# Down projection of a fused attention and FFN kernel: seven block products per 256 tokens in place of eight

## Chip, cores, metric

One core of one Trainium2 chip. The metric is the device time of that core in microseconds (us). Stage times come from the trace of one profiled execution per kernel.

## What is computed

Causal attention with a bias made from cumulated positions (batch 8, 8 heads, 576 positions, head size 64), whose output is the input of a gated FFN (4608 tokens, model width 512, inner width 1536). Inputs and output are fp32, the kernel computes in bf16. The change concerns the last line:

```python
def _moe_ref(x, w_gate, w_val, w_out):
    g = x @ w_gate
    silu = g * (1.0 / (1.0 + np.exp(-g)))
    val = x @ w_val
    return (silu * val @ w_out).astype(np.float32)
```

## The kernel before

The FFN runs over nine tiles of 512 tokens. A tile has a **gate stage** (twelve blocks of 128 inner columns, each with eight matmuls of 512 columns, a tanh on ScalarE and two VectorE products, `pp` and `ht`) and a **down stage** (four blocks of 128 tokens, each with twelve matmuls of 512 columns). Between the items of both stages (each `yield`) pieces of the attention of the next batch are slipped in: scores, masks on GpSimd, the product with V, casts and DMA issues on GpSimd, and copies of transposed keys and queries on VectorE. Tiles 7 and 8 have no attention left.

```python
        def ffn_items(tt):
            xt = XT[:, :, (tt % 3) * TT : (tt % 3 + 1) * TT]
            hts = []
            ...                                   # stores of the tile before
            for ft in range(NFT):                 # gate stage, NFT = 12
                ...                               # four matmuls into pg; tanh into th
                nc.vector.scalar_tensor_tensor(   # L578
                    pp, in0=th, scalar=1.0, in1=pg, op0=ALU.add, op1=ALU.mult
                )
                give(gbs)
                yield 1
                ...                               # four matmuls into pv
                ht = hpool.tile([128, TT], BF16, tag="ht", bufs=16, name="ht")
                nc.vector.tensor_mul(ht, pp, pv)  # L591
                give(vbs)
                hts.append(ht)
                yield 1
            for ts_ in range(4):                  # down stage
                ...                               # (the last block of all: two halves)
                ybs = take()
                py = view(ybs, DM)
                for ft in range(NFT):
                    nc.tensor.matmul(             # L620
                        py, hts[ft][:, ts_ * 128 : (ts_ + 1) * 128],
                        WO[ft // WKO][:, ft % WKO, :],
                        start=(ft == 0), stop=(ft == NFT - 1),
                    )
                    if ft % 4 == 3 and ft < NFT - 1:
                        yield 1
                ysb = yp.tile([128, DM], FP32, tag="y", name="ysb")
                nc.scalar.mul(ysb, py, 0.5)
                give(ybs)
                ...                               # store, one block late
```

Other work of VectorE and GpSimd in the gate stage that the argument needs:

```python
    split(h + 1, "k", nc.vector)          # keys, queries: copy of a DMA-transposed tile (L278, after: L281)
    cast_one(h + 2, "k", nc.gpsimd)       # 128x1152 fp32 to bf16 (after: L252)
    cast_v(bn, 0, nc.gpsimd)              # 128x512 fp32 to bf16 (after: L179)
    # masks of the scores on GpSimd: affine_select (after: L388, L393)
```

The softmax here doesn't subtract the row's maximum and nothing guards it: scores larger than these inputs give would overflow.

## Time and profile before

| | before |
|---|---|
| median time, three runs | 390.43 us (388.56 to 390.73) |
| span of the profile, granted clock | 388.6 us, 1.000 |
| TensorE, VectorE, GpSimd busy | 96%, 62%, 49% |
| tile 3: gate stage, down stage | 26.94, 13.31 us |
| last matmul to the end | 4.2 us |

A stage is measured from its first matmul to the first matmul of the next. Line numbers differ between the two kernels: L578, L591, L620 before are L605, L621, L668 after. The profile's lines stand in the prediction; the stage of one tile, with busy time (and instructions) of PE, PEld, DVE, ACT and POOL, then granted clock, DMA share and GB/s, is added here for tile 3.

```profile
164.23:191.17 26.94, 26.94 (x236) 14.96 (x232) 20.94 (x37) 16.28 (x33) 17.57 (x30) 1.00 0.83 198
191.17:204.47 13.30, 13.30 (x110) 7.24 (x108) 4.75 (x12) 7.19 (x15) 7.65 (x12) 1.00 0.96 226
```

TensorE has no gap in either stage. VectorE has 6 us free in the gate stage, 8.5 in the down stage.

### The profile page before, as it was taken

Reading aid. Unit: us, or ns where it says so; the run is one execution under the profiler, and the core shown is the slowest. Engines: PE = TensorE matmul, PEld = TensorE weight load, DVE = VectorE, ACT = ScalarE, POOL = GpSimd, SP = SyncE. Lnnn points to the kernel's source line nnn. Section 1 sums busy time; section 2 is a strip of 40 time slices with the busy share of each in tenths; the row PEclk is TensorE's granted clock in tenths of the full one; section 3 lists DMA queues with packets and bytes.
Section 4 is the critical chain, followed back from the end, with each engine's and each line's share of the span. In section 5 each row is a group of like instructions: output and inputs, shape, how many; then the busy total and the mean of one; then the engine's idle time right before and its main releaser. Section 6 shows DMA issues by size and latency. Waiting matters only on the chain.

```text
span 388.6 us, 7949 instructions
## 1 busy us (share of the span) xinstructions
PE 371.3 (96%) x3006; PEld 206.2 (53%) x3006; DVE 239.8 (62%) x431; ACT 214.5 (55%) x411; POOL 192.3 (49%) x329
## 2 busy tenths in 40 slices
PE   3779999999999999999999999999999999999995
PEld 3565556655555555555555555555555544444443
DVE  7676777468653786369735884488347625733750
ACT  7686877567646565566556655565464513323321
POOL 7683368656695756566656666576342220011001
PEclk9999999999999999999999999999999999999999
DMA  7999999996859998996789757964231222002002
GB/s 245 196 244 261 197 264 257 303 254 165 158 153 269 287 221 220 211 267 153 184 215 288 122 178 142 293 159 98 61 113 35 32 73 69 3 27 81 2 12 97
DMA packets 100534, 64.18 MB, mean 165 GB/s; under 512 B 81888, under 2 KB 85824, under 8 KB 100496
## 3 DMA queue, kind: packets, MB, share of 16 engines
q1 hardware_dynamic: 90816, 45.36, 50.3%
q0 software_dynamic: 9680, 18.32, 18.2%
q8 instruction: 23, 0.38, 0.4%
q14 instruction: 15, 0.12, 0.1%
HBM read 37.90 MB, written 19.86 MB: 149 GB/s over the span
## 4 chain that ended last, share of the span: by engine, by line
PE 82%; DVE 6%; DMA 5%; issue 3%; ACT 2%; POOL 0%; DVEq 0%; ACTq 0%; SPq 0%; POOLq 0%
PE bank L571 21%; PE bank L620 21%; PE bank L586 20%; PE bank L367 9%; PE bank L405 6%; DMA pk<-ks 2%; PE wide L367 2%; DVE pp L578 2%; ACT pt L380 1%; DVE ht L591 1%; DVE kq L320 1%; DMA kq<-HL 1%; PE one L405 1%; DMA XT<-xs 1%; DMA s_sb<-in_s_dram 1%
## 5 line engine op out<-in xcount | busy, mean ns | idle before, releaser
L380 ACT ACTIVATE pt<-bank 128x512 bf16<-128x512 f32 x224 | 104.1, 504 | 40.3 <-PE bank L367 28.5
L578 DVE SCALAR_TENSOR_TENSOR pp<-th,bank 128x512 bf16<-128x512 bf16 x108 | 74.1, 686 | 69.8 <-ACT th L576 69.0
L571 PE MATMUL bank<-XT,wg 128*128 128x512 bf16 x432 | 111.0, 379 | 1.1 <-DMA XT<-xs 0.5
L586 PE MATMUL bank<-XT,wv 128*128 128x512 bf16 x432 | 110.9, 379 | 0.2 <-DVE pp L578 0.2
L576 ACT ACTIVATE th<-bank 128x512 bf16<-128x512 f32 x108 | 64.5, 597 | 78.2 <-PE bank L571 73.9
L620 PE MATMUL bank<-wo,ht 128*128 128x512 bf16 x420 | 102.4, 379 | 0.0
L591 DVE TENSOR_TENSOR ht<-pp,bank 128x512 bf16<-128x512 bf16 x108 | 74.0, 685 | 8.8
L367 PEld LDWEIGHTS <-kq 128*128 128x128 bf16 x576 | 46.5, 99 | 40.3 <-issue 6.1
L367 PE MATMUL bank<-kq 128*128 128x128 bf16 (+4 forms) x504 | 65.9, 240 | 0.7 <-DVE ht L591 0.5
L383 POOL TENSOR_SCALAR_AFFINE_SELECT pt<-pt 128x512 bf16<-128x512 bf16 x64 | 41.0, 640 | 34.3 <-ACT pt L380 33.7
L571 PEld LDWEIGHTS <-wg 128*128 128x128 bf16 x432 | 38.3, 98 | 36.6 <-issue 1.2
L586 PEld LDWEIGHTS <-wv 128*128 128x128 bf16 x432 | 38.4, 98 | 35.1 <-issue 1.1
L620 PEld LDWEIGHTS <-ht 128*128 128x128 bf16 x420 | 37.1, 98 | 34.4
L405 PEld LDWEIGHTS <-pt 128*128 128x128 bf16 x960 | 41.5, 98 | 20.7
L439 POOL DMA_DIRECT2D xs<-ot x24 | 21.9, 913 | 60.8 <-DVE ot L422 60.8
L634 POOL DMA_DIRECT2D out_dram<-ysb x35 | 19.7, 562 | 60.9 <-ACT ysb L628 60.9
L628 ACT ACTIVATE ysb<-bank 128x512 f32<-128x512 f32 x35 | 20.9, 597 | 40.9 <-PE bank L620 39.7
L405 PE MATMUL bank<-vt,pt 128*128 128x65 bf16 x840 | 42.8, 194 | 0.0
L190 POOL DMA_DIRECT2D kq<-HL x52 | 31.3, 602 | 2.0 <-PE bank L571 1.6
L421 DVE RECIPROCAL rc<-bank 128x5 f32<-128x5 f32 x56 | 10.6, 190 | 34.4 <-PE bank L405 34.4
L422 DVE TENSOR_TENSOR ot<-bank,rc 128x320 bf16<-128x320 f32 x56 | 27.5, 491 | 1.9
L388 POOL TENSOR_SCALAR_AFFINE_SELECT pt<-pt 128x64 bf16<-128x64 bf16 x64 | 16.4, 256 | 21.3 <-ACT pt L380 21.1
(68 smaller groups left out, 211.1 us busy)
## 6 DMA issues: line engine op xcount, KB each, us to landing
out_dram<-ysb POOLq DMA_DIRECT2D x35, 256.0 KB, 3.3
rawk<-in_k_dram SPq DMA_DIRECT2D x15, 576.0 KB
rawq<-in_q_dram SPq DMA_DIRECT2D x15, 576.0 KB
rawv<-in_v_dram SPq DMA_DIRECT2D x32, 256.0 KB
xs<-ot POOLq DMA_DIRECT2D x24, 160.0 KB, 3.9
ks<-ck SPq DMA_DIRECT2D x11, 288.0 KB
qs<-cq SPq DMA_DIRECT2D x11, 288.0 KB
wg<-in_moe_w_gate_dram POOLq DMA_DIRECT2D x2, 768.0 KB, 11.6
```

Of the source, the lines that this page charges most:

```text
L190: engs[hh].dma_start(KQ[hb % 2][r][r0 : r0 + 4, :, e * S : (e + 1) * S], HL[bh : bh + 1, :, :, :],)
L367: nc.tensor.matmul(sc[:, o : o + w], T[:, 1, e * S + 128 * tj : e * S + 128 * (tj + 1)], T[:, 0, e * S + lo : e * S + hi], start=True, sto ...
L380: nc.scalar.activation(pt[:, c0 : c0 + W], sc[:, 0:W], AF.Exp, scale=0.125)
L383: nc.gpsimd.affine_select(pt[:, 1088:1600], pt[:, 1088:1600], pattern=[[0, 4], [1, 128]], compare_op=ALU.is_ge, fill=zreg, base=0, channel ...
L405: nc.tensor.matmul(av[:, bi * (D + 1) : (bi + 1) * (D + 1)], pt[:, c0 : c0 + 128], VT[b % 2][:, tj, h, :], start=(tj == 0), stop=(tj == bi),)
L422: nc.vector.tensor_mul(ot[:, :, e * D : (e + 1) * D], av3[:, :, 0:D], rc[:, :, None].to_broadcast([128, NCH, D]),)
L571: nc.tensor.matmul(pg, WG[j][:, c, f0 : f0 + 128], xt[:, c, :], start=(c == 0), stop=(c == 3),)
L576: nc.scalar.activation(th, pg, AF.Tanh, scale=0.5)
L578: nc.vector.scalar_tensor_tensor(pp, in0=th, scalar=1.0, in1=pg, op0=ALU.add, op1=ALU.mult)
L586: nc.tensor.matmul(pv, WV[j][:, c, f0 : f0 + 128], xt[:, c, :], start=(c == 0), stop=(c == 3),)
L591: nc.vector.tensor_mul(ht, pp, pv)
L620: nc.tensor.matmul(py, hts[ft][:, ts_ * 128 : (ts_ + 1) * 128], WO[ft // WKO][:, ft % WKO, :], start=(ft == 0), stop=(ft == NFT - 1),)
```

## The change

Each down stage of tiles 1 to 8 is split into two groups of 256 tokens, and each group is a 2x2 block product (token halves by pairs of inner blocks by output halves) done with seven products in place of eight, in Winograd's form of Strassen's scheme. A product is six matmuls of 256 columns. TensorE gets 84 matmuls of 256 columns per tile instead of 48 of 512, an eighth less. The price is sums of operands: of the weights once, of `ht` in every tile (two additions on VectorE, one subtraction in place on GpSimd per pair of blocks), and sums of results.

```diff
+                if k2 == 1 and tt > 0:               # gate stage, after every second ht
+                    su = PTP[0].tile([128, 3, HT], BF16, tag="su", bufs=NP, name="su")
+                    nc.vector.tensor_add(su[:, 0:2, :], hp[:, 0:2, :], hp[:, 2:4, :])         # L628
+                    nc.vector.tensor_add(su[:, 2, :], hp[:, 0, :], hp[:, 3, :])               # L629
+                    nc.gpsimd.tensor_sub(hp[:, 1:3, :], hp[:, 1:4:2, :], hp[:, 0:3:2, :])     # L630
...
+                if ts_ == 3:                          # end of tile 0: sums of the weights
+                    for j in range(2):
+                        weight_sums(j)                # three VectorE operations of 768 elements
+                        weight_differences(j)         # two, in place in WO
...
+        def down_seven(tt, hps, sus):
+            for g in range(2):
+                PB[g] = take()
+                product(P[g][:, 0:HD], True, False, lambda p: hps[p][:, 0, cols], ...)       # raw
+                product(P[g][:, HD:DM], False, False, lambda p: hps[p][:, 3, cols], ...)     # raw
+                nc.scalar.copy(s3, P[g][:, 0:HD])
+                nc.vector.tensor_add(DE[g][:, 0, :], s3, P[g][:, HD:DM])
+                QB[g] = take()
+                product(Q[g][:, HD:DM], True, True, lambda p: hps[p][:, 1, cols], ...)       # difference
+                product(Q[g][:, 0:HD], False, False, lambda p: sus[p][:, 2, cols], ...)      # sum
+                nc.vector.tensor_add(DE[g][:, 1, :], DE[g][:, 0, :], Q[g][:, 0:HD])
+            for g in range(2):
+                product(P[g][:, 0:HD], False, True, lambda p: sus[p][:, 0, cols], ...)
+                product(P[g][:, HD:DM], False, True, lambda p: sus[p][:, 1, cols], ...)
+                nc.scalar.copy(Y[g][:, 1:3, :]..., P[g])
+                nc.gpsimd.tensor_sub(DE[g], DE[g], Y[g][:, 1:3, :])                           # L707
+                product(Q[g][:, 0:HD], False, True, lambda p: hps[p][:, 2, cols], ...)
+                nc.vector.tensor_add(Y[g][:, 0:4:3, :], DE[g], Q[g]...)
+                ...                                   # two stores
...
-    yp = ctx.enter_context(tc.tile_pool(name="yp", bufs=3))
+    yp = ctx.enter_context(tc.tile_pool(name="yp", bufs=2))
```

Cut: the buffers of the scores go from eight to five after the start to make room, and the pace at which attention is slipped in is adapted.

## The prediction

> **What bounds the kernel now.** I read the page's busy lines first, then the chain of work that ended last, then the groups, then VectorE's timeline inside one tile.
>
> ```profile
> PE 371.3 (96%) x3006; PEld 206.2 (53%) x3006; DVE 239.8 (62%) x431; ACT 214.5 (55%) x411; POOL 192.3 (49%) x329
> PE 82%; DVE 6%; DMA 5%; issue 3%; ACT 2%; POOL 0%; DVEq 0%; ACTq 0%; SPq 0%; POOLq 0%
> 342.91 10.36 PE bank L620 x48
> 381.76 2.63 PE bank L604 x24
> ```
>
> The first line is busy time, the second the chain by engine, the last two are pieces of that chain in order of time (start, us, what). TensorE sets the time: its longest waits after the start-up are below 0.6 us in total for each pair of lines. One down projection of a tile (512 tokens) is 48 matmuls of 512 columns in 10.36 us, so 215.8 ns each. The last piece of the last tile, 24 matmuls of 256 columns in 2.63 us, gives 109.6 ns each: a half-width matmul costs half, and the weight loads (98 ns each) stay hidden. So fewer columns on TensorE is the right currency, provided that nothing makes TensorE wait.
>
> ```profile
> L578 DVE SCALAR_TENSOR_TENSOR pp<-th,bank 128x512 bf16<-128x512 bf16 x108 | 74.1, 686 | 69.8 <-ACT th L576 69.0
> L591 DVE TENSOR_TENSOR ht<-pp,bank 128x512 bf16<-128x512 bf16 x108 | 74.0, 685 | 8.8
> 204.60:231.50 26.90, 26.90 (x232) 14.94 (x229) 21.01 (x37) 16.22 (x33) 17.45 (x30) 1.00 0.79 181
> 231.50:244.90 13.40, 13.40 (x110) 7.25 (x108) 5.59 (x12) 7.30 (x16) 7.83 (x13) 1.00 0.88 192
> ```
>
> The last two lines are busy time by engine (PE, PEld, DVE, ACT, POOL) in the two stages of tile 4: gate and value, then down projection. VectorE's 62% is uneven: 21.0 of 26.9 us in the first stage and 5.6 of 13.4 in the second. The change puts most of its VectorE work in the full stage. How full that is, the timeline shows:
>
> ```profile
> 225.63 0.69 DVE L578 SCALAR_TENSOR_TENSOR pp<-th,bank 128x512 bf16<-128x512 bf16 x1
> 226.42 0.69 DVE L591 TENSOR_TENSOR ht<-pp,bank 128x512 bf16<-128x512 bf16 x1
> 227.02 0.68 DVE L578 SCALAR_TENSOR_TENSOR pp<-th,bank 128x512 bf16<-128x512 bf16 x1
> 227.62 0.19 DVE L421 RECIPROCAL rc<-bank 128x5 f32<-128x5 f32 x1
> ...
> 230.94 0.69 DVE L578 SCALAR_TENSOR_TENSOR pp<-th,bank 128x512 bf16<-128x512 bf16 x1 [0.62 <-ACT th L576]
> 232.18 0.68 DVE L591 TENSOR_TENSOR ht<-pp,bank 128x512 bf16<-128x512 bf16 x1
> ```
>
> An instruction that needs the one before it starts 0.79 us after it (225.63 to 226.42); one that does not starts after 0.60 us. From 218.4 to 230.3 there is no idle time at all; in the whole stage the idle gaps in brackets add to 3.2 us (0.31, 0.90, 0.37, 0.70, 0.30, 0.62).
>
> **What the Trainium skill says.** (1) "TensorE: Matmul & The Clock Gate", Back-to-back issue gap: 262 cycles for 256 columns, so 109 ns; the trace has 109.6. (2) "VectorE: DVE Perf Modes", The perf-mode tier table: a two-tensor operation on bf16 in SBUF reaches two elements per cycle, with a PSUM operand one. The trace confirms the second (686 ns for 512); of the first it has no instance. Estimate with the fixed part that 686 - 512/0.96 = 153 ns leaves: 0.42 us for 512 elements, 0.29 us for 256. (3) "GPSIMD Engine Reference", 3.1: a two-input addition at 2.6 cycles per element, 4497 ns for 2048; estimate 1.15 us for 512. The trace has only one-input work there (a cast of 1152 in 1.15 us), so this is untested. (4) "SBUF - State Buffer", Who interferes with whom: a VectorE instruction with two SBUF inputs contends with a GpSimd instruction that reads SBUF. The before trace has none such in the FFN, but its SBUF copies show what contention does:
>
> ```profile
> L278 DVE COPY kq<-pk x22: 442/496/1634, 83.7 to 277.3; 64x1152 bf16<-64x1152 bf16 x22
> ```
>
> Minimum, median, maximum in ns: the same copy takes 442 to 1634.
>
> **The change, part by part.**
> *TensorE.* Per tile 2 x 7 x 6 = 84 matmuls of 256 columns, 84 x 109.6 = 9.20 us in place of 10.36: 1.16 us per tile, for 8 tiles **-9.3 us**, 2.4% of 390. That is the ceiling.
>
> *VectorE and GpSimd in the gate stage.* Each of six pairs of f blocks adds on VectorE one addition of 512 that needs the product before it (the 0.19 us more of a dependent start, then 0.33 us of occupancy: 0.42 less the overlap of 0.09 seen above) and one of 256 (0.20): 0.72 us. Then GpSimd subtracts in place (1.15 us), after the two additions have read. Products 1 and 2 need the raw ht of blocks 10 and 11, product 3 needs the last subtraction.
>
> *Tiles with attention beside them (1 to 5), tile 4 as example.* Five pairs before the last ht add 3.6 us. Going through the gaps in order: the first pair vanishes in the 0.90 gap, the second in the 0.70, the next three meet only the 0.62: lag 1.56 us at the last ht, which ends at 232.86 + 1.56 = 234.4. TensorE begins the down stage at about 231.5; product 1 (0.66), 0.23 of attention, and five matmuls of product 2 bring it to 232.9: it waits 1.5 us. The additions end at 235.15, the subtraction at 236.4; TensorE is at product 3's sixth matmul at 235.5: 1.0 us more. So 2.5 us per tile, **+12.5 us** for five. Not counted: contention of twelve additions with GpSimd, which is busy for 65% of this stage before it gets 7 us more.
> *Tile 6* has VectorE gaps that swallow the additions (5 us of idle between 286 and 312), not the last latency: **+1.5**.
> *Tiles 7 and 8*, without attention: TensorE takes 3.45 us for a pair (16 x 215.8 ns), VectorE 0.79 + 0.60 + 0.79 + 0.60 + 0.72 = 3.50. The rates match, but at the end product 2 waits about 0.6 us for the last ht and product 3 about 1.3 for the subtraction: 1.9 each, **+3.8**.
>
> *VectorE and ScalarE in the down stage* have room; four of eight banks stay open but reuse in that stage is slow. Nothing counted. *Weight sums* once, ten VectorE operations of 768 elements between tiles 0 and 1, some 6 us of which 2 come after the last matmul that reads the weights: **+0.5**.
>
> *The end.* Before, TensorE's end at 384.4 was followed by a half-width move of 0.42 us and a store: 388.6, so 4.2 us. Now the last group needs a copy on ScalarE (0.60), a subtraction of 512 fp32 elements on GpSimd (1.15), which also waits behind two store issues of the first group (0.54 each), then an addition of 0.69 on VectorE and two issues: about 7.5 us. **+3.3.**
>
> Sum: -9.3 + 12.5 + 1.5 + 3.8 + 0.5 + 3.3 = **+12.3**, 402.7 us. Contention would add up to 1 us per tile; against that, waits inside the gate stage or on a bank replace part of the wait at its end and are counted once only, and a hand replay of queues tends to overcount. I take **401 us**.
>
> **Rivals.**
> *A: the gain arrives.* If GpSimd is quicker than estimated and VectorE's additions fit, the waits shrink to the pure latency and only the end costs: -9.3 + 3 + some 2 to 4 = 386 to 388. For it: the order of the products puts those with raw operands first, as cover, and attention lies between the products. Against it: the cover is 1.4 us, and the chain last ht, two additions, subtraction is already 0.69 + 0.7 + 1.15 = 2.5 us without any lag. Even so it does not reach 2%.
> *B: GpSimd becomes the bound.* It gets 6 x 1.15 + 2 x 1.15 = 9.2 us per tile on top of 25.2 of 40, in strict order, and waits for VectorE's lagging additions; behind it come the casts and issues that feed the next heads' keys and queries. If those land late, VectorE's copies (which wait up to 4.2 us for their transposes already) hold up the gate chain: another 1 to 3 us per tile, 407 to 418. For it: casts of 1.15 us and blocked copies. Against: GpSimd's inputs are prepared about a batch of heads ahead.
> *C: PSUM.* Four banks held in the down stage leave four for attention, and TensorE waits for banks: a microsecond per tile. Against it: one score piece per 0.9 us needs some 1.5 us of a bank.
>
> **Range and chances.** The low end is A, the high end the sum with most of B: 386 to 413. Faster by over 2% means below 382.6, which would need nearly no wait and a free end: 0.04. Within 2% (to 398.2) needs the waits at two thirds of my count or less: 0.40. Slower: 0.56.
>
> **What would show it.** TensorE's matmuls in the down projection at 109 to 110 ns apart inside a product (step 1). Idle of TensorE put down to ht on VectorE before product 2 and to the GpSimd subtraction before product 3, 1 to 3 us per tile (steps 2, 3). The two additions at 0.42 and 0.29 us, the subtraction at 1.15. VectorE over 85% busy in gate stages. About 7.5 us from TensorE's end to the span's end. I am wrong if TensorE stays gapless in the down stages, which would mean that the additions or the subtraction cost far less than estimated; or if the biggest waits are on banks or on the keys' transposes.

## The result

| | before | after |
|---|---|---|
| median (four runs each, side by side) | 389.88 us (388.56 to 390.73) | 433.19 us (431.40 to 433.66) |
| span of the profile, granted clock | 388.6 us, 1.000 | 431.8 us, 0.965 |
| TensorE, VectorE, GpSimd busy | 96%, 62%, 49% | 87%, 74%, 62% |

The changed kernel is correct and **slower by 11%**: ratio 1.1101 (1.1063 to 1.1139). Here and below a ratio is from fast runs alone, so not quite the ratio of the medians quoted; in brackets is its 95% interval. Executions over 1.5% slower than the fastest of the same kernel are left out of the means. The prediction was 401 us with a range of 386 to 413, so it had the likelier direction and was 32 us short.

The page of the kernel after: busy time, granted clock by fortieths of the span, and the chain that ended last by engine.

```profile
PE 376.1 (87%) x3282; PEld 236.9 (55%) x3282; DVE 318.6 (74%) x584; ACT 211.9 (49%) x411; POOL 269.5 (62%) x394
...
PEclk9879999879899989899999999999999999999997
...
PE 46%; DVE 29%; issue 8%; POOL 8%; DMA 4%; ACT 2%; SPq 0%; DVEq 0%; POOLq 0%; ACTq 0%
```

In the chain TensorE fell from 82% to 46%, VectorE rose from 6% to 29%, GpSimd from 0 to 8%. The clock, full throughout before, has dips.

**Where the 43.2 us are.** Stage lengths from the two traces:

| us | gate: before, after | down: before, after | down: TensorE idle, after |
|---|---|---|---|
| tile 0 | 30.26, 29.97 | 17.81, 17.81 | |
| tile 1 | 29.55, 41.18 | 14.11, 13.59 | 0.80 |
| tile 2 | 27.10, 33.26 | 13.31, 15.97 | 2.20 |
| tile 3 | 26.94, 30.82 | 13.31, 14.44 | 2.19 |
| tile 4 | 26.94, 31.77 | 13.31, 14.44 | 2.19 |
| tile 5 | 26.94, 30.82 | 13.31, 14.44 | 2.19 |
| tile 6 | 25.75, 25.75 | 10.64, 10.96 | 1.16 |
| tile 7 | 21.39, 21.59 | 10.36, 10.61 | 1.09 |
| tile 8 | 20.72, 20.72 | 10.55, 11.19 | 1.50 |
| last matmul to end | 4.23 | 10.01 | |

Gate stages of tiles 1 to 5: **+30.4**. Gate stages of 6 to 8: +0.2. Down stages of 1 to 5: +5.5, of 6 to 8: +1.2. End: +5.8. The head and tile 0: +0.1. So the loss is mostly not where the products are but in the stage before, where only their operands are made, and only where attention runs beside it.

Tile 3 of the kernel after, the same columns as before:

```profile
184.26:215.08 30.82, 28.11 (x237) 15.35 (x234) 29.12 (x50) 16.64 (x35) 23.80 (x34) 1.00 0.73 184
215.08:229.53 14.45, 12.26 (x144) 10.49 (x142) 7.21 (x18) 6.55 (x16) 10.75 (x16) 1.00 0.78 182
```

VectorE is busy for 29.12 of 30.82 us, 8.2 more than before. Ten of the tile's twelve additions fall in this stage. By their minimum durations (424 and 276 ns) they account for 3.5 of these; they took 6.7. Most of the rest isn't theirs: without any sum (x1 below) the stage already has 23.7 us of VectorE, as a query copy, an attention output and an addition of results more fall in it than before. The groups by tile form show which instructions last longer (busy us, mean ns, idle before and releaser):

```profile
L630 POOL TENSOR_TENSOR ht<-ht 128x512 bf16<-128x512 bf16 x48 | 55.3, 1153 | 67.8 <-DVE su L628 61.3 <-PE bank L598 6.3
L628 DVE TENSOR_TENSOR su<-ht 128x512 bf16<-128x512 bf16 x48 | 26.2, 546 | 1.7
L629 DVE TENSOR_TENSOR su<-ht 128x256 bf16<-128x256 bf16 x48 | 25.7, 535 | 0.0
L281 DVE COPY kq<-pq 64x1152 bf16<-64x1152 bf16 x22 | 21.6, 981 | 0.3
```

```profile
L628 DVE TENSOR_TENSOR su<-ht x48: 424/426/2158, 93.2 to 412.5; 128x512 bf16<-128x512 bf16 x48
L629 DVE TENSOR_TENSOR su<-ht x48: 276/284/4033, 93.5 to 412.9; 128x256 bf16<-128x256 bf16 x48
```

The second fence is the source view (minimum, median, maximum ns). Half of the additions run at the estimated speed; a few take up to fourteen times that. Of the 48 of 256 elements, five begin while a mask or a cast runs on GpSimd and take 2.37 to 4.03 us; the other 43 begin while none runs and take 276 to 287 ns. The additions together are 18.3 us longer than 48 times their minima (26.2 - 20.4 and 25.7 - 13.2). The longest case, on VectorE's timeline and on GpSimd's (start us, us, instruction):

```profile
108.28 0.48 DVE L628 TENSOR_TENSOR su<-ht 128x512 bf16<-128x512 bf16 x1
108.69 4.03 DVE L629 TENSOR_TENSOR su<-ht 128x256 bf16<-128x256 bf16 x1
112.65 0.95 DVE L281 COPY kq<-pk 64x1152 bf16<-64x1152 bf16 x2
```

```profile
108.45 0.81 POOL L388 TENSOR_SCALAR_AFFINE_SELECT pt<-pt 128x512 bf16<-128x512 bf16 x1
109.23 1.14 POOL L630 TENSOR_TENSOR ht<-ht 128x512 bf16<-128x512 bf16 x1
110.33 1.13 POOL L252 CAST cq<-rawq 128x1152 bf16<-128x1152 f32 x1
111.42 1.16 POOL L179 CAST vt<-rawv 128x512 bf16<-128x512 f32 x2
112.54 0.27 POOL L393 TENSOR_SCALAR_AFFINE_SELECT pt<-pt 128x64 bf16<-128x64 bf16 x1
```

The addition of 256 elements starts while a mask runs on GpSimd and ends with an unbroken row of GpSimd instructions. The subtraction released by the first addition (L628) overtakes the second (L629): the change puts its own GpSimd work into the way of its own VectorE work. The next product `pp` (L605) starts only at 113.63, and TensorE's longest wait for one, 2.7 us up to 114.37, is what follows from it.

**TensorE's waits** (what waits, for what; us in total, times, longest):

```profile
PE bank L668 <- POOL ht L630: 10.8, 8, 1.8
...
PE bank L372 <- DVE pp L605: 5.5, 5, 2.7
PE bank L598 <- DVE XT L467: 4.3, 1, 4.3
PE bank L372 <- DVE kq L281: 4.0, 3, 1.3
...
PE bank L598 <- DVE ht L621: 2.8, 5, 0.6
PE bank L668 <- DVE ht L621: 2.4, 6, 0.6
PE bank L613 <- DVE ht L621: 2.2, 1, 2.2
```

The first line is the down stage: once per tile the product of differences waits for the subtraction, 1.8 us in tiles 2 to 5. The waits at L598, L613 and L372 lie in the gate stages and are for VectorE; in tile 3 they are 1.34 us for a query copy, 0.60 for `ht`, 0.51 for `pp`. None of these matmuls reads `pp` or `ht`: there TensorE waits for an accumulator bank in PSUM that the lagging product on VectorE has yet to read. These and smaller ones make the 2.7 us of the 3.9 that TensorE is idle there; the other 1.2 show as longer matmul records (28.11 us busy in place of 26.94; x1 has 27.16), and since matmul ends are modelled I don't read more into that. The 2.2 us at L613, in tile 2, are not the sums' doing: before that `ht` VectorE waited for the late DMA transpose of a key, and without any sum (x1) the same two waits are 3.63 and 2.14 us.

```profile
153.82 0.92 DVE L281 COPY kq<-pk 64x1152 bf16<-64x1152 bf16 x2 [2.76 <-DMA pk<-ks]
155.51 1.56 PE L613 MATMUL bank<-XT,wv 128*128 128x512 bf16 x4 [2.19 <-DVE ht L621]
```

The single 4.3 us stands at the start of tile 1: VectorE's copy of the next input (XT) came behind the ten weight operations. After it, TensorE ran at half the clock:

```profile
84.18:91.01 6.83, 5.62 (x27) 2.80 (x27) 3.96 (x9) 2.31 (x5) 2.14 (x3) 0.50 0.24 84
```

Three more stretches at 0.50, each 3.41 us, begin at 114.9, 155.9 and 172.9, within or just after waits of 2.7, 2.2 and 1.8 us. Half of 17.07 us is what the four cost at most, 8.5 us (estimate). (A fifth, 6.83 us from 19.32, lies in the head, which is 0.4 us longer than before.)

**By cause** (estimate, from the tables): fewer columns -9.3; TensorE waiting in the down stages 13.3; wait for the weights at tile 1 4.3; half clock 8.5; end 5.8; and in the gate stages of tiles 1 to 5 what is left of 30.4 after that wait and 6.8 of half clock, 19.3, or 3.9 per tile; some 3 of them stand in x1 too, without any sum. Another 1.3 is spread. Sum 43.2.

### The profile page after: what moved, and what is told of

It reads as the page before. It is cut to its first block, busy times and chain, and to the rows that moved or that the text cites. A ratio compares the mean times of both kernels' runs of the same rounds, so it can differ in the third digit from the quotient of the medians.

```text
span 431.8 us, 8783 instructions
## 1 busy us (share of the span) xinstructions
PE 376.1 (87%) x3282; PEld 236.9 (55%) x3282; DVE 318.6 (74%) x584; ACT 211.9 (49%) x411; POOL 269.5 (62%) x394
## 4 chain that ended last, share of the span: by engine, by line
PE 46%; DVE 29%; issue 8%; POOL 8%; DMA 4%; ACT 2%; SPq 0%; DVEq 0%; POOLq 0%; ACTq 0%
PE bank L598 11%; PE bank L668 11%; PE bank L613 9%; DVE ht L621 8%; DVE pp L605 7%; PE bank L372 5%; PE bank L410 4%; DVE su L628 4%; DVE su L629 3%; DVE kq L281 3%; POOL ht L630 3%; POOL kq L193 2%; PE bank L640 2%; DMA pk<-ks 2%; PE wide L372 2%
## 5 line engine op out<-in xcount | busy, mean ns | idle before, releaser
L385 ACT ACTIVATE pt<-bank 128x512 bf16<-128x512 f32 x224 | 105.9, 504 | 65.8 <-PE bank L372 57.3
L598 PE MATMUL bank<-XT,wg 128*128 128x512 bf16 x432 | 113.9, 386 | 8.6 <-DVE XT L467 4.3
L613 PE MATMUL bank<-XT,wv 128*128 128x512 bf16 x432 | 112.6, 384 | 2.8 <-DVE ht L621 2.2
L630 POOL TENSOR_TENSOR ht<-ht 128x512 bf16<-128x512 bf16 x48 | 55.3, 1153 | 67.8 <-DVE su L628 61.3
L605 DVE SCALAR_TENSOR_TENSOR pp<-th,bank 128x512 bf16<-128x512 bf16 x108 | 73.7, 682 | 14.6 <-ACT th L603 14.0
L621 DVE SCALAR_TENSOR_TENSOR ht<-pp,bank 128x512 bf16<-128x512 bf16 x108 | 74.1, 686 | 10.0 <-PE bank L613 0.5
L372 PE MATMUL bank<-kq 128*128 128x128 bf16 (+4 forms) x504 | 69.3, 244 | 10.0 <-DVE pp L605 5.5
L372 PEld LDWEIGHTS <-kq 128*128 128x128 bf16 x576 | 48.0, 102 | 41.6 <-issue 15.7
L598 PEld LDWEIGHTS <-wg 128*128 128x128 bf16 x432 | 39.4, 99 | 42.6 <-issue 9.5
L613 PEld LDWEIGHTS <-wv 128*128 128x128 bf16 x432 | 38.8, 99 | 40.0 <-issue 5.6
L410 PEld LDWEIGHTS <-pt 128*128 128x128 bf16 x960 | 43.8, 100 | 21.1 <-issue 6.4
L668 PE MATMUL bank<-WS,ht 128*128 128x256 bf16 x192 | 27.7, 274 | 10.8 <-POOL ht L630 10.8
L707 POOL TENSOR_TENSOR de<-de,ysb 128x512 f32<-128x512 f32 x16 | 20.7, 1296 | 16.9 <-ACT ysb L705 16.8
L711 DVE TENSOR_TENSOR ysb<-de,bank 128x512 f32<-128x512 f32 x16 | 11.0, 689 | 25.1 <-POOL de L707 14.8
L668 PEld LDWEIGHTS <-su 128*128 128x128 bf16 x288 | 27.0, 99 | 3.3
```

Of the source, the lines that this page charges most:

```text
L372: nc.tensor.matmul(sc[:, o : o + w], T[:, 1, e * S + 128 * tj : e * S + 128 * (tj + 1)], T[:, 0, e * S + lo : e * S + hi], start=True, sto ...
L385: nc.scalar.activation(pt[:, c0 : c0 + W], sc[:, 0:W], AF.Exp, scale=0.125)
L410: nc.tensor.matmul(av[:, bi * (D + 1) : (bi + 1) * (D + 1)], pt[:, c0 : c0 + 128], VT[b % 2][:, tj, h, :], start=(tj == 0), stop=(tj == bi),)
L598: nc.tensor.matmul(pg, WG[j][:, c, f0 : f0 + 128], xt[:, c, :], start=(c == 0), stop=(c == 3),)
L605: nc.vector.scalar_tensor_tensor(pp, in0=th, scalar=1.0, in1=pg, op0=ALU.add, op1=ALU.mult)
L613: nc.tensor.matmul(pv, WV[j][:, c, f0 : f0 + 128], xt[:, c, :], start=(c == 0), stop=(c == 3),)
```

## The experiments

The theory after the result: the sums of `ht` cost little by their own length; they cost by what VectorE and GpSimd make each other wait for in a gate stage that leaves VectorE little room, and by the wait for the last subtraction. Rivals: VectorE's load alone (rival "load"), or late transposes and keys (the prediction's B). The runs of the kernel before lay at 388.3 to 393.0 us (medians 389.2 to 389.6).

### 1 to 4: parts of the sums taken away (wrong results on purpose)

x1_nosums, no sum of `ht` at all; x2_noport, the additions replaced by VectorE copies of as long a nominal duration that read PSUM; x3_subonly, only the subtraction; x4_addonly, only the additions.

```diff
 x1, x3, x4: lines L628, L629 and/or L630 out; the products take hps[p][:, 0] or [:, 3] where a sum is missing
 x2:
-                    nc.vector.tensor_add(su[:, 0:2, :], hp[:, 0:2, :], hp[:, 2:4, :])
-                    nc.vector.tensor_add(su[:, 2, :], hp[:, 0, :], hp[:, 3, :])
+                    nc.vector.tensor_copy(su[:, 0, :], pv[:, 0:HT])
+                    nc.vector.tensor_copy(su[:, 1, 0:128], pv[:, 0:128])
 (and give(vbs), which frees the PSUM bank, moves behind the copies)
```

> All additions and subtractions of operands (ht) left out, the seven products take raw blocks: wrong result on purpose. Theory (the sums on VectorE and GpSimd cost the time, in the gate stage by VectorE operations that wait for the shared SBUF port, and at its end by the latency of the last sums): the gate stages of tiles 2 to 5 go back to 27 to 27.5 us (33.3, 30.8, 31.8, 30.8 in the changed kernel), their down stages to 12.2 to 12.5 us (16.0, 14.4, 14.4, 14.4); tile 1 keeps some 8 us of loss from the weight sums and the half clock after them, the end keeps 10 us. Time 390 - 9.3 + 8 + 6 = about 395. Rival (the product order, the open PSUM banks and the smaller pool of pt hold TensorE up, whatever the sums do): the gate or down stages stay longer, time above 410.

> The two additions of each pair are replaced by two VectorE operations of the same nominal length (0.42 and 0.29 us) that read PSUM and no SBUF[...]; GpSimd's subtraction stays. Wrong result on purpose. Theory (blocking on the shared port): none of these operations is longer than 0.45 us, the gate stages of tiles 2 to 5 shrink by 2 to 3.5 us each and the half-clock stretches after long waits go, time 410 to 420. Rival (VectorE's plain load of 0.7 us per pair in a full stage): the gate stages stay within 1 us, time 428 to 435.

> GpSimd's subtractions stay, VectorE's additions are left out. Wrong result on purpose. Theory: only the copies of keys and queries on VectorE can be blocked now; gate stages of tiles 2 to 5 within 1 us of 27.5, and in the down stage TensorE waits for the last subtraction still, 0.5 to 1.5 us per tile; time 398 to 405. Rival (GpSimd's strict queue is the cause: subtractions delay masks, casts and DMA issues): gate stages of 29 us or more, time above 412.

> VectorE's additions stay, GpSimd's subtractions are left out. Wrong result on purpose. Theory: the additions are blocked by casts and masks alone, mean of the 256-element one 0.3 to 0.45 us in place of 0.535; the wait for the subtraction in the down stage goes, that for ht stays; gates of tiles 2 to 5 at 28.5 to 30; time 408 to 418. Rival (the additions' load by itself): gates at 30.5 or more and time 422 or more.

| | median | ratio to before | tile 3: gate, down |
|---|---|---|---|
| after | 433.19 | 1.1101 | 30.82, 14.44 |
| x1 no sums | 400.59 | 1.0303 (1.0235 to 1.0372) | 27.16, 11.90 |
| x4 additions only | 409.63 | 1.0512 (1.0461 to 1.0562) | 28.67, 12.95 |
| x3 subtraction only | 417.80 | 1.0727 (1.0652 to 1.0802) | 29.00, 13.98 |
| x2 subtraction and copies from PSUM | 420.33 | 1.0796 (1.0754 to 1.0839) | 28.97, 15.63 (3.4 of it at half clock) |

Tile 3 without sums (x1), where the columns saved show by themselves:

```profile
171.52:198.68 27.16, 27.16 (x237) 15.08 (x234) 23.72 (x42) 16.44 (x35) 20.77 (x34) 1.00 0.79 211
198.68:210.58 11.90, 11.90 (x143) 10.65 (x142) 5.71 (x14) 6.54 (x16) 7.32 (x10) 1.00 0.92 185
```

27.16 + 11.90 = 39.06 against 26.94 + 13.30 = 40.24 before: 1.18 us won per tile, as predicted (1.16), and no idle time of TensorE. So the scheme works on TensorE, and the order of the products, the open banks and the smaller pool of score buffers (x1's rival) cost nothing there; the sums of `ht` cost 32.6 us of the whole (433.2 - 400.6). What x1 still loses, 5 us more than I had forecast, lies in tile 1 (gate 36.95, the wait for the weights is still there), in tile 2 (31.06, the late transpose with half clock behind it) and at the end (10.0). Its gate stages of tiles 1 to 5 are 12.4 us longer than before; less the wait for the weights (4.3) and half clock (5.1 at most) 3.0 remain, so some 16 of the 19.3 us above are the sums' (estimate).

The gate stage of tile 3 with the subtraction alone (x3) and with the additions alone (x4):

```profile
177.02:206.02 29.00, 27.63 (x237) 15.15 (x234) 25.63 (x42) 16.54 (x35) 24.25 (x35) 1.00 0.70 192
176.67:205.34 28.67, 27.64 (x238) 15.20 (x235) 26.99 (x50) 16.55 (x35) 20.50 (x33) 1.00 0.79 207
```

The copies of x2 and its gate stage:

```profile
L627 DVE CAST su<-bank x48: 417/418/421, 90.7 to 399.8; 128x256 bf16<-128x256 f32 x48
L628 DVE CAST su<-bank x48: 280/281/283, 91.0 to 400.1; 128x128 bf16<-128x128 f32 x48
```

```profile
177.19:206.16 28.97, 27.61 (x238) 15.14 (x235) 26.91 (x51) 16.54 (x35) 24.22 (x35) 1.00 0.73 197
```

The same number of VectorE operations at the same unblocked length, never one longer than 421 ns, and the gate stage is 28.97, as long as x3's without any (29.00). So in tile 3 **the load of the additions costs nothing; the 1.8 us that they add beside the subtraction (30.82 - 29.00) come with the two SBUF operands**: TensorE's waits of 0.51 and 0.60 us for `pp` and `ht` are gone in x2, that for the query copy stays (1.31). Two limits: x2 also lets the subtraction start without waiting for an addition, and no run separates that from blocking. And tile 3 is the clearest case: in tile 5 x2's gate stage is 0.53 us longer than x3's (28.98, 28.45), and in tiles 2 and 4 x2's own copies hold a bank for which TensorE waits 2.7 and 1.7 us. So "load" falls as the main cost, not to nothing everywhere. x2's total is at the upper edge of my forecast (410 to 420), and half clock, which I had expected to go, is still there twice.

The rest of the gate stage's 3.66 us (30.82 - 27.16) is the subtraction's: 1.84 by itself (29.00 - 27.16). There TensorE waits for a query copy (1.31 us); these take 1115 ns in the mean in x3 and 876 in x1. Additions alone (x4) cost 1.5: the ten in this stage take 5.7 us in place of 3.5, with only the masks and casts on GpSimd that were there before.

In the whole kernel additions alone cost 9.0 us and the subtraction alone 17.2; together they cost 32.6, more than the sum of 26.2. For x3 I had expected much less, 398 to 405: the subtraction on GpSimd, which I took to run aside, is the dearer of the two. The total is what its rival (GpSimd's strict queue holds up masks, casts and issues) had forecast, above 412. But the rival's path doesn't show: in x3's gate stages of tiles 2 to 5 every wait of TensorE names VectorE, none GpSimd, and VectorE waits no longer for key transposes than in x1 (6.7 and 7.3 us in all).

### 5 to 7: one remedy each (right results)

x5_rawfirst puts all four products of raw operands first, as cover for the last subtraction. x6_weights makes the weights' sums among tile 0's down blocks and the in-place differences one by one in tile 1's gate stage. x7_end moves the last tile's fp32 subtractions to VectorE and its stores to two other queues.

```diff
 x5:
-            for g in range(2):   # raw 0, raw 3, difference, sum
+            for g in range(2):   # raw 0
+            for g in range(2):   # raw 3, s3, DE
+            for g in range(2):   # difference, sum
 x6:
-                if ts_ == 3: all sums and differences
+                if ts_ < 2: weight_sums(ts_)
+                if tt == 1 and ft % 2 == 0 and ft < 8: weight_difference(ft // 2)
 x7:
-                nc.gpsimd.tensor_sub(DE[g], DE[g], Y[g][:, 1:3, :])
+                (nc.vector if tt == NTT - 1 else nc.gpsimd).tensor_sub(DE[g], DE[g], Y[g][:, 1:3, :])
-                        nc.gpsimd.dma_start(
+                        eng = (nc.sync, nc.scalar)[i] if tt == NTT - 1 else nc.gpsimd
+                        eng.dma_start(
```

> The four products with raw operands (both token groups) come first, then the four that need a subtraction or a sum; nothing else changes, result right. Theory (the wait at the end of the gate stage is latency of the last ht and the last subtraction, so cover removes it): idle of TensorE in the down stages, 13.3 us over the eight tiles in the changed kernel, falls below 4 us, and the subtraction is no longer what TensorE waits for; gate stages unchanged; time 421 to 425. Rival (VectorE and GpSimd are simply behind by more than the cover): the idle only moves to a later product, time above 429.

> The weight sums, ten VectorE operations in a row between tiles 0 and 1, are spread: the sums into the plain down projection of tile 0, the four in-place differences one by one into the gate stage of tile 1. Result right. Theory: the 4.3 us in which TensorE waits for the copy of XT behind them and the 6.8 us at half clock after it (3.4 us lost) go: tile 1's gate stage from 41.2 to 34 to 36 us, time 424 to 427. Rival (tile 1 is late for the same port blocking as the others): within 2 us of 433.

> In the last tile alone the subtraction of fp32 blocks goes to VectorE and the stores to two other issue queues. Result right. Theory (the end is a chain copy, GpSimd subtraction behind store issues, addition, store issues): from TensorE's last matmul to the end 5 to 6 us in place of 10.0, time 428 to 429. Rival (the stores' landing sets it): less than 2 us gained.

x5: 417.35 us, 1.0700 (1.0669 to 1.0730), 15.8 less than the change. Its gate stage is as before the remedy, its down stage 1.8 shorter:

```profile
177.24:208.12 30.88, 28.12 (x237) 15.35 (x234) 29.23 (x51) 16.65 (x35) 23.87 (x34) 1.00 0.78 197
208.12:220.76 12.64, 12.08 (x143) 10.56 (x142) 8.07 (x18) 6.65 (x16) 11.10 (x16) 1.00 0.73 177
```

TensorE's idle time in the down stages fell from 13.3 to 2.8 us, and tiles 6 to 8 became faster than before the change (35.27, 30.94, 30.23 against 36.39, 31.75, 31.27). So the prediction's wait at the end of the gate stage was real. It is 10.5 of the 15.8 us (I had forecast 421 to 425); another 5.1 is half clock, which lasts 6.83 us here in place of 17.07, and only one of the stretches that went, 3.41 us, lay behind a wait for the subtraction.

x6: 428.09, 1.0975 (1.0916 to 1.1035). The 4.3 us wait and the half clock behind it are gone, tile 1's gate stage is 36.7 (41.2); both are a little short of the forecast, and tile 0's down stage, which now holds the sums, is 1.0 longer. x7: 428.29, 1.0989 (1.0928 to 1.1050); from the last matmul to the end 6.1 us (10.0). Each gives back about 5 us, x7 3.9 of it at the end itself. Most of that 3.9 is the last stores: from the last addition to the end it is 3.8 us, as before the change, in place of 6.5 with the stores issued on GpSimd.

### 8: key and query copies on ScalarE

> The 44 copies of keys and queries from the transposed tile go from VectorE to ScalarE. Result right. Theory (VectorE's time in the gate stages is the bound, partly because such copies are blocked by GpSimd): gate stages of tiles 2 to 5 shrink by 2 to 4 us each, time 415 to 424. Rival (ScalarE's strict order: a copy that waits for its transpose holds up tanh and exp): gate stages not shorter, time 430 or more.

```diff
-                eng.tensor_copy(KQ...)       # split, VectorE
+                nc.scalar.copy(KQ...)
```

444.93 us (438.15 to 446.04), three of the four runs slow; the size is inconclusive, but nothing speaks for a gain (the one fast run took 438.15). In the profile, of a slow run, the gate stages of tiles 2 to 5 took 32.4 to 37 us: on ScalarE the copies wait in order for the DMA transposes, up to 4.3 us, and hold the tanh up.

```profile
ACT kq L281 <- DMA pk<-ks: 9.2, 4, 4.3
```

Here the prediction's rival B (late transposes) is real; in the change itself it shows once, in the 2.2 us wait of tile 2.

### 9, 10, 12: move the sums

x9_deferred: raw products first, and in tiles 1 to 5 all sums on VectorE in the down stage (the subtraction, su2, then su0 = su2 - d2, su1 = su2 + d1). x10_best: the same from tile 2 on, with the remedies of x6 (one tile later) and x7. x12_subdve: raw first, the subtraction on VectorE in the gate stage.

```diff
 x9:
-                    (the three sums after every second ht)
+            def later(k):                    # k = 0 to 5, after the first six products, three pairs of blocks each
+                    if k < 2: nc.vector.tensor_sub(h[:, 1:3, :], h[:, 1:4:2, :], h[:, 0:3:2, :])
+                    elif k < 4: nc.vector.tensor_add(u[:, 2, :], h[:, 0, :], h[:, 3, :])
+                    else: nc.vector.tensor_sub(u[:, 0, :], u[:, 2, :], h[:, 2, :]); nc.vector.tensor_add(u[:, 1, :], u[:, 2, :], h[:, 1, :])
 x12:
-                    nc.gpsimd.tensor_sub(hp[:, 1:3, :], ...)
+                    nc.vector.tensor_sub(hp[:, 1:3, :], ...)
```

> Raw products first as before, and in tiles 1 to 5 the sums leave the gate stage: all of them on VectorE during the four raw products of the down stage, GpSimd's subtraction gone there. Result right. Theory (the loss in the gate stages is VectorE's additions and copies blocked by GpSimd there): gate stages of tiles 3 and 5 back to 27.2 to 27.6 us (30.9 with raw products first), down stages at 12 to 14 us; time 400 to 408 against 417 with raw products first alone. Rival (VectorE's load needs the time wherever it is): the down stages grow by as much as the gate stages shrink, time above 413.

> Attempt at the best version: seven products from tile 2 on, raw products first, sums deferred in tiles 2 to 5, weight differences one by one in the gate stage of tile 2, a shorter end. Result right. If each of these removes its own loss, tiles 2 to 8 keep most of 1.1 us each and the end costs 1 us: 383 to 388, just ahead of the kernel before at 389.5. If the deferred sums are blocked in the down stage: 390 to 397.

> Raw products first, and the subtraction moves from GpSimd to VectorE in the gate stage: more load on VectorE (some 0.35 us per pair), less on GpSimd. Result right. Theory (blocking by GpSimd counts more than VectorE's load): the gate stages of tiles 3 and 5 do not get longer than 30.9 us but shorter, 29 to 30.5, time 408 to 415 against 417. Rival (load): gates of 32 us and more, time 422 or more.

x9: 413.28, 1.0607 (1.0587 to 1.0628); only about 4 us below x5, a miss of my 400 to 408 and just what the rival "load" had forecast (above 413). The gate stages of tiles 2, 4 and 5 are back at 27.16, that of tile 3 at 27.95, but the time went to the down stage (tile 3, 12.64 in x5):

```profile
204.08:219.90 15.82, 13.58 (x144) 10.43 (x143) 12.89 (x38) 6.64 (x16) 7.76 (x10) 1.00 0.93 184
```

VectorE is now busy for 12.89 of 15.82 us here, and TensorE idles 2.2. The room that the averages show isn't there when the sums must come before the products that follow within the same 12 us.

x10: 404.02 (one of its four runs, 410.71, slow), 1.0367 (1.0339 to 1.0395). I had expected it near or below the kernel before; a miss: the remedies' gains don't make up for the sums.

x12: 419.39, 1.0761 (1.0733 to 1.0789), between its theory (408 to 415) and its rival (422 or more). VectorE does more and tile 3's gate stage is **shorter** than x5's, 30.04 against 30.88 (tile 5: 30.03 against 30.89):

```profile
179.93:209.97 30.04, 27.75 (x233) 15.35 (x234) 28.47 (x55) 16.64 (x35) 20.61 (x34) 1.00 0.78 198
```

That again speaks for blocking over load in the gate stage. The total didn't follow: tile 1's gate stage was 44.3, and the down stages of tiles 7 and 8 got 1.1 us of idle time.

### 11, 13: seven products only where there is room

x11_last3: seven products in tiles 6 to 8 alone, where the gate stages lost nothing; raw first, weights spread over tiles 5 and 6, the new end. x13_last3b: the same with four output buffers of half the size in the plain tiles.

```diff
 x11: if tt < 6: down_plain; sums of ht if tt >= 6
 x13:
-                ysb = yp.tile([128, 2, DM], FP32, tag="y", name="ysb")
+                if ts_ % 2 == 0:
+                    ysb2 = yp.tile([128, 2, DM], FP32, tag="y", name="ysb")
+                ysb = ysb2[:, ts_ % 2, :]
```

> Seven products in tiles 6 to 8 alone, where little or no attention lies beside them; raw products first, shorter end; tiles 0 to 5 as in the kernel before. Result right. Theory: tiles 6, 7, 8 gain 1.1, 0.8 and 1.0 us, the end costs 0.5 to 1 us: 387 to 388.5, within 1% of the kernel before. Rival (something else in the new layout, as the smaller pool of pt or the packed ht, costs time in tiles 1 to 5): above 392.

> Seven products in tiles 6 to 8 alone as in x11_last3, with four output blocks in flight in the plain tiles in place of two. Result right. Theory (in x11_last3 ScalarE waited for an output buffer in tiles 2 to 5): these tiles go back to 40.3 us each from 40.9 to 41.9, time 386 to 387.5, faster than the kernel before by 0.5 to 0.9%. Rival (something else in the layout): 390 or more.

x11: 391.36, 1.0047 (1.0024 to 1.0071). Tiles 6 to 8 gained (35.27, 30.29, 30.03), but tiles 2 to 5 took 40.9 to 41.9 in place of 40.3, though their work is that of before. The change had taken one of three output buffers away; the loss shows in the gate stages that follow (28.05 in tile 3, 26.94 before), not in the down stages (13.31 as before).

x13: **387.27** (386.65 to 389.32, six runs) against 389.50, 0.9944 (0.9905 to 0.9982), correct. Tiles 2 to 5 are back at 40.25, tiles 6 to 8 take 35.28, 30.42, 30.03 (3.7 less than before), the end 1.7 more. The clock is full. This version beats the kernel before by half a per cent, which is clear of the noise but below the 2% at which the record speaks of a difference, and about what three of eight tiles can give: 3 x 1.2 less 1.7.

### 14, 15: take the long blocks away

In the change the subtraction is released by the first addition and so comes to lie before the second. x14_swap swaps the two additions, so that the subtraction waits for both. x15_fixed: swap, raw first, spread weights and the new end together.

```diff
-                    nc.vector.tensor_add(su[:, 0:2, :], hp[:, 0:2, :], hp[:, 2:4, :])
                     nc.vector.tensor_add(su[:, 2, :], hp[:, 0, :], hp[:, 3, :])
+                    nc.vector.tensor_add(su[:, 0:2, :], hp[:, 0:2, :], hp[:, 2:4, :])
                     nc.gpsimd.tensor_sub(hp[:, 1:3, :], ...)
```

> The two additions of each pair change places, nothing else: the 512-element one, which the subtraction waits for, now comes second. Same work, same load, result right. Theory (GpSimd's unbroken row holds the port, and the pair's own subtraction closes the gap): GpSimd now has to wait for the second addition, which breaks its row; no addition waits longer than some 2.2 us, the sum of the additions' blocked time (18 us) falls by a third or more, gate stages of tiles 3 and 5 lose 0.8 to 2 us; time 422 to 430. Rival (the additions are blocked by casts and masks whatever the order): within 2 us of 433.

> Raw products first, weight sums spread, shorter end and swapped additions together, seven products in tiles 1 to 8 as in the changed kernel. Result right. If the losses add up: 433 - 16 - 5 - 5 - 6 = 401, range 398 to 406; what is left above 390 - 9.3 is then GpSimd's subtraction against VectorE's copies, and blocking by casts and masks in the gate stages of tiles 1 to 5.

x14: 433.08, 1.1108 (1.1063 to 1.1153): no difference. The mechanism was met:

```profile
L628 DVE TENSOR_TENSOR su<-ht x48: 291/292/2024, 92.2 to 411.6; 128x256 bf16<-128x256 bf16 x48
L629 DVE TENSOR_TENSOR su<-ht x48: 410/418/846, 92.5 to 411.8; 128x512 bf16<-128x512 bf16 x48
```

The longest addition is 2.02 us in place of 4.03, the excess over the minima about half (9.1 us in place of 18.3), and tile 3's gate stage 30.40 in place of 30.82. But the subtraction now starts later, its wait in the down stages grew by 0.2 each, two of these waits (tiles 3 and 4) have 3.4 us at half clock behind them, and the total stayed. I had expected 422 to 430: a miss. The longest single blocks are striking and real, but the order of the two additions isn't what sets the total.

x15: 410.80, 1.0538 (1.0490 to 1.0587), above the 398 to 406 forecast, which counted 6 us for the swap. The single gains of x5, x6 and x7 taken from the change's time would give 433.2 - 15.8 - 5.1 - 4.9 = 407.4; so they add up but for 3 us, and 21 us remain above before.

## Why the prediction was wrong, point by point

- **TensorE's gain: right.** 84 half-width matmuls take 9.2 us, and tile 3 without sums is 1.18 us shorter (x1).
- **Durations of the sums: right where nothing is in the way.** 424 and 276 ns for the additions (predicted 0.42 and 0.29), 1153 ns for the subtraction (1.15).
- **Down stages: right in kind and nearly in size.** Of the predicted sum, -1.16 + 2.5 per tile 1 to 5 makes +6.7; measured +5.5. Tiles 6 to 8: -3.5 + 1.5 + 3.8 = +1.8; measured +1.2. The waits are those named, but split the other way: 1.5 for the last `ht` and 1.0 for the subtraction were predicted in tile 4, 0.4 and 1.8 measured. x5 takes most of them away. 1.7 of the +5.5 is half clock in tile 2.
- **The step that failed is "Not counted: contention of twelve additions with GpSimd".** The replay for tile 4 went through VectorE's gaps with unblocked durations and let the lag end in one wait at the last `ht`, none inside the gate stage (it also left out a gap of 4.18 us that ends 1.6 us into the stage); later "Contention would add up to 1 us per tile" was netted to zero. Measured: the gate stages of tiles 1 to 5 are 30.4 us longer, 19.3 without the weights' wait and the half clock, some 16 of them from the sums. For tile 3 the runs split 3.66 us into 1.84 for the subtraction alone and 1.82 for the additions beside it, which cost nothing there when they read PSUM (x1, x2, x3). The prediction had quoted the line that warned of it (a copy of 442 to 1634 ns), and then didn't ask what a blocked instruction makes wait in a stage with 6 us of room: TensorE, for banks that VectorE frees late and for query copies. It also put the subtraction's cost in the down stage alone; x3 shows it at work in the gate stage too.
- **Weights: wrong in size.** Predicted +0.5. Measured a wait of 4.3 us with 6.83 us at half clock behind it; spreading them gives back 5.1 us (x6). The ten operations were in front of the copy of tile 1's input on VectorE; I counted only the wait for their results.
- **The end: wrong in size.** Predicted +3.3, measured +5.8; x7 shortens it by 3.9. The term too small is the last two store issues on GpSimd and what follows them: 6.5 us from the last addition to the end, for which the predicted 7.5 leaves some 4 after its other terms.
- **The clock: not foreseen.** Waits that TensorE didn't have before are dear twice, some 8.5 us here (estimate). The clock records of the traces begin and end in steps of 3.413 us. Over all 17 traces, from 34 us to just before the last matmul, 26 such windows at full clock have 2.0 us or more without a matmul, and all 26 have half clock behind them; of 19 with 1.7 to 1.95 us 5 have, of some 1,700 with less only 3 (in x9 and x10). So what counted here is the idle time within one window: of two waits of 1.81 us in the kernel after, that of tile 2 lies with 1.62 us in one window beside another of 0.38, 2.0 together, and has half clock behind it; that of tile 3 stands alone in its window and has none.
- **Rivals.** A is out. B named GpSimd and blocked copies, which belong to the cause, but by late transposes, which show once (tile 2, 2.2 us of wait with 3.4 us at half clock behind it, and in x1 as well); its 407 to 418 was also short. C, banks held in the down stage, doesn't show, and x1, with the same banks, has no wait in tiles 3 and 5. But the gate stages' waits for `pp` and `ht` (5.5, 2.8 and 2.2 us in the list) are for banks that VectorE frees late, a form of wait that the prediction didn't count.

**What stays open.** Why a blocked addition gets in at some boundaries between GpSimd instructions and waits through several at others. Why three windows with less than 1.6 us of idle time (x9, x10) were followed by half clock. How much of the additions' cost is the later start of the subtraction. What sets tile 1's longer gate stage apart when the weights are spread. And x14 halves the blocked time of the additions without a gain, so how much of the 32.6 us of the sums hangs on single blocks and how much on the two engines' shared pace isn't split for the whole kernel; it is split only for tile 3.

## What to carry to other kernels

Before moving arithmetic from a full engine to engines that look half empty, take their room in the very stage, with the durations they have beside each other, and ask what stands behind a blocked instruction: here, on VectorE at 78% of the stage before and 94% after, it is the chain that feeds the full engine. Measure such a change without its price first (x1 took one kernel and showed 3% lost without any sum), and apply it only to the stages with room, as x13 does. Where a product needs freshly made operands, put all products of raw operands first.

## What the Trainium skill lacked or had wrong

- "SBUF — State Buffer", Who interferes with whom: the page says that a VectorE instruction with two SBUF inputs contends with a GpSimd instruction that reads SBUF, and of the shared ports "Whoever issues first gets the shared pair for the whole instruction; the other fully blocks". This agrees in kind (additions of two SBUF tiles stretched from 0.276 to 4.03 us; copies from PSUM, x2, never over 0.421). It lacks that the wait can last over several instructions: five GpSimd instructions in a row, none over 1.15 us, four of which began after the addition.
- "TensorE: Matmul & The Clock Gate", Part 1: half clock in windows of about 3.4 us agrees (0.50 for 3.41 or 6.83 us). So does the window that runs by itself: the four stretches of the kernel after begin 30.72, 40.96 and 17.07 us apart, which is 9, 12 and 5 times 3.413. It names idle gaps of over about 3.4 us as the cause in a running kernel (and, for a second case, short idle times without a figure); here waits of 2.7, 2.2 and 1.8 us had half clock behind them. What share of a window must be idle, the page doesn't say; here 2.0 us of 3.413 always sufficed (26 of 26), and 1.7 to 1.95 at times (5 of 19).
- "GPSIMD Engine Reference", 3.1: the estimate of 1.15 us for a two-input operation of 512 elements holds (1.153 in bf16); in fp32 it was 1.296. The page says that the SBUF interfaces are shared with VectorE, but has no figure for what such an operation costs there: 1.84 us of a stage of 27 for the five that fall in it (x3).
- "VectorE: DVE Perf Modes", The perf-mode tier table: the estimates of 0.42 and 0.29 us hold as minima (0.424, 0.276), not beside GpSimd (means 0.546 and 0.535).
